# An FFT-style convolution on one core: 32-pixel x chunks, a first weight group from one weight copy, earlier plane bursts, and one queue for the last scratch reads

## The chip, the cores and the metric

The kernel runs on one core of a Trainium2 chip. The metric is the device time of one execution in microseconds (us). A program on one core has no second die to compare with, so a run counts as slow when it is over 1.5% above the fastest run of the same kernel, and only the fast runs are compared. Each profile is one further execution with the hardware profiler on; its span is some 1 to 2 us shorter than the timed runs.

## The reference

The reference is a circular 7x7 convolution done with Fourier transforms.

```
x: [1, 224, 224, 96] bfloat16      w: [7, 7, 96, 96] bfloat16
wp = pad(w, to 224 x 224)
Xf = rfft2(x as float32, axes=(1, 2));  Wf = rfft2(wp as float32, axes=(0, 1))
Yf = einsum('bhwi,hwio->bhwo', Xf, Wf)
y  = irfft2(Yf, s=(224, 224), axes=(1, 2)) as bfloat16
```

## The kernel before

The kernel transforms along the rows only, in blocks of 28 rows with a real transform of 34 points (17 frequencies). Along the other axis it convolves directly. Its stages are these:

- **x banks.** Rows of x (tile `xn`) are multiplied by a transform matrix `Fm` on TensorE, and the result is copied to `xf` (96 channels on partitions). The width is cut into seven tiles of 32 pixels, t = 0 to 6.
- **Weight banks.** w (tile `wq`) is multiplied by `Em` and copied to `WF`. This is done in six groups of frequencies. `wq` holds two copies of w on 49 partitions each, shifted by half the output channels. One matmul on 98 partitions then makes two output channels. The third weight slot of each frequency is the difference of the other two, formed on VectorE (`w_sub`).
- **Planes.** VectorE forms sums and differences of `xf` (tile `J`) for three frequencies at a time. Such a burst is `jit(t, g)`. There are two plane buffers, and a third in the two-tile phase.
- **Rounds.** `b_round(t, s)` runs 33 convolution matmuls of 96 columns (22 for frequency 0), combines them on ACT, VectorE and POOL (`u`, `v`, `yf`) and writes to a scratch tensor in DRAM (`scr`).
- **Output products.** The scratch is read back (`tt`), multiplied by the inverse matrix `Gm`, copied to `yo` and written out.

Tiles 0 and 1 run interleaved, tile 1 four rounds behind (the two-tile phase). Tiles 2 to 6 follow one by one. Other stages' matmuls are slipped into the rounds as "jobs", each list with a window of slots, two slots to a round. The parts that the change touches, with cuts marked:

```python
NXN = 4                                   # x buffers, each PXC = 16 pixels (of each phase pair) wide
# ... start: what is loaded, in program order; DE is the SP queue
load_rows(xh_bufs[0], 0, W - PAD, PAD)
load_x(0)
load_rows(xh_bufs[1], 1, W - PAD, PAD)
load_x(1)
load_w(0, DE)                             # first copy of w
for c in range(2, NXN):
    load_x(c)
# ... 24 warm matmuls; later, after the sine tables have been started:
load_w(1, SE)                             # second copy of w, from the ACT queue
# ... a weight bank of any group, the first one (full) included
for k in range(hb):                       # hb = 4
    o = ob * hb + k
    TE.matmul(pv_[:, k], lhsT=wqx[0:PW2, o:o + 127 * C + 1:C], rhs=ev, start=True, stop=True)
# ... the order of work at the start
a0 = a_jobs(0)                            # 28 x banks
p0 = prep_jobs(0)                         # 12 weight banks
for _ in range(16):
    a0.pop(0)()
warm(2)
for _ in range(4):
    p0.pop(0)()
while p0 or a0:
    if p0:
        p0.pop(0)()
    for _ in range(2):
        if a0:
            a0.pop(0)()
for f in jit(0, 0):
    f()
# ... when weight differences and plane bursts are formed in the two-tile phase
for gi in range(1, len(PGRP)):
    b0 = PGRP[gi][0]
    add(max(0, 2 * b0 - 10), 2 * b0 - 4 if gi > 1 else 2, prep_jobs(gi))
    for h, (r, t) in enumerate(((b0 - 4, 1), (b0 - 2, 0)) if gi > 1 else ((0, 0), (1, 0))):
        wsubs.setdefault((r, t if r >= LAG else 0), []).append(w_sub(gi, h))
for g in range(len(JGB)):
    g0 = JGB[g][0]
    # ...
    r1 = LAG + g0 - 1
    bursts[(r1, 0 if r1 < NS else 1)] = (1, g)
bursts[(NS + LAG - 1, 1)] = (2, 0)        # first planes of tile 2, in the very last round
for r in range(NS + LAG):
    if r == NS:
        add(2 * r, 2 * (r + LAG) - 2, a_jobs(2))
    # ...
    now = jit(*now) if now else []
    if (r, t) in wsubs:
        now.extend(wsubs.pop((r, t)))     # planes first, then weight differences
# ... tiles 2 to 6: the older tile's output products start in slot 3
km = 3 + -(-(k1 - 3) * nold // (nold + nnew))
add(3, km, cj[:nold])
# ... after the last round
load_b(1, SE, 1)
load_b(2, DE, 1)
```

## Time and profile before

| | before |
|---|---|
| runs, us | 304.72, 305.99, 301.41 (median 304.72) |
| span of the profiled execution | 301.7 us |
| mean granted TensorE clock | 0.954 |
| TensorE busy | 271.0 us (90%) |

The lines that carry the reading stand in the prediction below. To read them, start from the busy row and the clock row of the slices. Where TensorE has a gap, look at the clock just behind it. Then ask the list of TensorE's waits who ended the gap. Nearly every instruction carries the line of one helper (L82), so the groups are told apart by tile names, not by lines. The moment at which the convolution could first start ends the expensive start of this kernel. It is seen in the instructions in order of time (start, duration, engine, line, operation, tiles and form, and in brackets the idle time before and who ended it):

```profile
19.40 1.85 PE L82 MATMUL pb<-wq 98*128 98x100 bf16 x20 [6.63 <-DMA wq<-in_w_dram]
...
27.69 0.50 PE L82 MATMUL pb<-WF,xf 96*128 96x96 bf16 x8 [0.76 <-DVE WF L82]
```

The first weight product waits 6.63 us for w, and round 0 of the convolution starts at 27.69 us.

### The profile page before, as it was taken

What the parts mean: (1) busy time and instruction counts of PE and PEld (TensorE: products, weight loads), DVE (VectorE), ACT (ScalarE), POOL (GpSimd) and SP (SyncE); (2) the same over time, 40 slices, a digit from 0 to 9 for tenths busy, and PEclk for the clock granted to TensorE, in tenths of its full rate; (3) what the DMA queues carried; (4) which work ended last, traced back from release to release, by engine and by line L of the source; (5) the groups of instructions that cost most, each with busy time, mean ns of one, the idle gap of its engine ahead of it and who ended that gap; (6) DMA issues with size and microseconds to landing.
All of it is one profiled execution on the core that took longest, in us unless ns stands there. A gap on an engine that the chain in (4) does not pass through costs nothing. (4 is left out here: it accounts for less than half of the span.)

```text
span 301.7 us, 11617 instructions
## 1 busy us (share of the span) xinstructions
PE 271.0 (90%) x4826; PEld 244.3 (81%) x4826; DVE 241.6 (80%) x517; ACT 188.6 (62%) x466; POOL 88.4 (29%) x124
## 2 busy tenths in 40 slices
PE   8548969999989689999999999999999999899863
PEld 3448969999979688998989897989888988688742
DVE  7828998999898858788988889788988799578713
ACT  2427957665612744777688857878688864666113
POOL 6811001322434311322422423422423416222100
PEclk9958979999979977999999999999999999799999
DMA  7983223111121549877757773887549543957825
GB/s 184 187 194 99 54 72 112 41 41 43 42 81 41 169 132 206 230 204 215 215 169 193 212 211 125 230 232 200 166 135 220 145 137 105 242 168 189 196 79 182
DMA packets 46084, 46.01 MB, mean 152 GB/s; under 512 B 33658, under 2 KB 35238, under 8 KB 45934
## 3 DMA queue, kind: packets, MB, share of 16 engines
q1 hardware_dynamic: 44462, 42.61, 51.9%
q10 hardware_dynamic: 1570, 2.67, 3.3%
q8 instruction: 38, 0.62, 0.9%
q14 instruction: 14, 0.11, 0.1%
HBM read 23.92 MB, written 21.33 MB: 150 GB/s over the span
## 5 line engine op out<-in xcount | busy, mean ns | idle before, releaser
L82 PE MATMUL pb<-WF,J 96*128 96x96 bf16 x2898 | 172.9, 209 | 6.1 <-DVE J L82 5.6
L82 PEld LDWEIGHTS <-J 96*128 96x128 bf16 (+1 forms) x2910 | 147.3, 99 | 22.2 <-issue 10.1
L82 POOL TENSOR_TENSOR yf<-v,u 128x384 bf16<-128x384 f32 x74 | 74.2, 1017 | 176.9 <-issue 103.9
L82 ACT CAST xf<-pb 96x408 bf16<-96x408 f32 (+1 forms) x138 | 61.2, 468 | 12.8 <-PE pb L82 9.8
L82 ACT CAST yo<-pb 84x384 bf16<-84x384 f32 (+1 forms) x139 | 59.5, 479 | 9.5 <-PE pb L82 8.6
L82 PE MATMUL pb<-WF,xf 96*128 96x96 bf16 x952 | 61.6, 209 | 4.1 <-DVE WF L82 3.5
L82 DVE TENSOR_TENSOR J<-xf 96x1824 bf16<-96x1824 bf16 (+1 forms) x84 | 57.1, 719 | 0.0
L82 PEld LDWEIGHTS <-xf 96*128 96x128 bf16 x952 | 48.5, 99 | 4.5 <-issue 3.6
L82 PE MATMUL pb<-Fm,xn 118*128 118x136 bf16 x448 | 49.7, 233 | 1.2 <-DVE u L82 0.8
L82 PE MATMUL pb<-tt,Gm 102*84 102x384 bf16 (+1 forms) x144 | 36.8, 334 | 2.1 <-DMA tt<-scr 1.5
L82 ACT CAST WF<-pb 96x480 bf16<-96x480 f32 (+1 forms) x57 | 28.6, 563 | 10.3 <-PE pb L82 10.2
L82 PEld LDWEIGHTS <-xn 118*128 118x128 bf16 x448 | 32.3, 103 | 2.3 <-issue 1.9
L82 PE MATMUL pb<-wq 98*128 98x120 bf16 (+1 forms) x288 | 24.6, 236 | 6.8 <-DMA wq<-in_w_dram 6.6
L82 PEld LDWEIGHTS <-wq 98*128 98x128 bf16 x288 | 21.6, 151 | 7.3 <-issue 7.3
L82 DVE TENSOR_TENSOR J<-J 96x912 bf16<-96x912 bf16 (+1 forms) x42 | 25.0, 596 | 0.0
L82 DVE TENSOR_TENSOR yf<-v,u 128x384 bf16<-128x384 f32 x37 | 21.2, 572 | 1.3
L82 DVE CAST xf<-pb 96x408 bf16<-96x408 f32 (+1 forms) x34 | 16.3, 508 | 1.2 <-PE pb L82 0.8
L82 PEld LDWEIGHTS <-Gm 102*84 102x84 bf16 (+1 forms) x144 | 11.5, 115 | 4.4 <-DMA tt<-scr 1.6
L82 DVE CAST WF<-pb 96x480 bf16<-96x480 f32 (+1 forms) x15 | 9.0, 615 | 7.4 <-PE pb L82 7.2
L82 PE MATMUL pb<-wu 128*128 128x512 bf16 (+1 forms) x52 | 12.0, 392 | 1.1 <-DVE ct L82 1.1
L82 PEld LDWEIGHTS <-wu 128*128 128x128 bf16 (+1 forms) x52 | 6.2, 122 | 6.9 <-issue 3.4
L82 DVE CAST tt<-pb 112x384 bf16<-112x384 f32 x8 | 4.2, 554 | 8.2 <-PE pb L82 7.9
(390 smaller groups left out, 216.0 us busy)
## 6 DMA issues: line engine op xcount, KB each, us to landing
xn<-in_x_dram SPq DMA_DIRECT2D x28, 336.0 KB
scr<-yf SPq DMA_DIRECT2D x30, 288.0 KB
tt<-scr SPq DMA_DIRECT2D x24, 288.0 KB
out_dram<-yo SPq DMA_DIRECT2D x24, 252.0 KB
tt<-scr SPq DMA_DIRECT2D x12, 192.0 KB
out_dram<-yo SPq DMA_DIRECT2D x12, 168.0 KB
scr<-yf SPq DMA_DIRECT2D x6, 192.0 KB
wq<-in_w_dram SPq DMA_DIRECT2D x1, 864.0 KB
```

The costliest lines, as they stand in the source:

```text
L82: r = fn(*a, **k)
```

## The change

Its intent is to shorten the start (half the weight bytes before the first weight product), to take waits on `WF` and `J` out of the two-tile phase, and to free the ACT queue of a scratch read at the end. The diff, cut to its core (VectorE's copy into `Fm` also moves ahead of the second sine, and the x banks are cut from the wider chunks):

```diff
-NXN = 4
+NXN = 2                                   # two buffers of 32 pixels
 ...
 load_rows(xh_bufs[0], 0, W - PAD, PAD)
 load_x(0)
+load_w(0, DE)
 load_rows(xh_bufs[1], 1, W - PAD, PAD)
-load_x(1)
-load_w(0, DE)
-for c in range(2, NXN):
-    load_x(c)
+load_x(1, 0, 1)
+load_x(1, 1, 1)
+load_w(1, DE)                             # second copy last, same queue
 ...
-    for _ in range(8):                    # 24 warm matmuls
+    for _ in range(4):                    # 12
 ...
-GE.memset(wqx[0:PW2, C * C + 2 * NSLOT * NTAP:], 0.0)
-load_w(1, SE)
+SE.copy(out=wpad, in_=wu[0:PW2, 0:1].to_broadcast(list(wpad.shape)))
 ...
+if full:                                  # first group: 49 partitions, 8 matmuls of 50 columns a bank
+    ev = Em[0:PW, 0, ...]
+    for k in range(NB):
+        TE.matmul(pv_[:, k], lhsT=wqx[0:PW, o:o + 127 * C + 1:C], rhs=ev, start=True, stop=True)
 ...
-for _ in range(16): a0.pop(0)()
-warm(2)
-for _ in range(4): p0.pop(0)()
-while p0 or a0: ...
-for f in jit(0, 0): f()
+for _ in range(14): a0.pop(0)()
+for _ in range(4):
+    p0.pop(0)()
+    warm(1)
+for k in range(14):
+    a0.pop(0)()
+    if k in (6, 9): p0.pop(0)()
+for f in jit(0, 0): f()
+while p0:
+    p0.pop(0)()
+    if len(p0) % 2: warm(1)
 ...
-for h, (r, t) in enumerate(((b0 - 4, 1), (b0 - 2, 0)) ...
+for h, (r, t) in enumerate(((max(b0 - 4, 2), 1), (b0 - 2, 0)) ...
 r1 = LAG + g0 - 1
+if g == len(JGB) - 1:
+    r1 = NS                               # tile 1's last burst: round 18 -> 17
-bursts[(NS + LAG - 1, 1)] = (2, 0)
+bursts[(NS + LAG - 2, 1)] = (2, 0)        # tile 2's first burst: round 20 -> 19
-add(2 * r, 2 * (r + LAG) - 2, a_jobs(2))
+add(2 * r, 2 * (r + LAG - 2) + 1, a_jobs(2))
-now.extend(wsubs.pop((r, t)))
+now = wsubs.pop((r, t)) + now if r < 2 else now + wsubs.pop((r, t))
 ...
-km = 3 + -(-(k1 - 3) * nold // (nold + nnew))
-add(3, km, cj[:nold])
+k0 = 12 if t == 2 else 3
+km = k0 + -(-(k1 - k0) * nold // (nold + nnew))
+add(k0, km, cj[:nold])
-load_b(1, SE, 1)
+load_b(1, DE, 1)
```

More of the change, by code (lines that the diff above doesn't have):

```diff
@@ L146 @@
     assert sum(KB) == 128
-    xn_bufs = [cpool.tile([R, PXC * C + 32], BF16, name=f"xn{i}") for i in range(NXN)]
+    xn_bufs = [cpool.tile([R, 2 * PXC * C + 32], BF16, name=f"xn{i}") for i in range(NXN)]
     wtmp_cm = tc.tile_pool(name="wtmp", bufs=1, side="right")
@@ L159, with load_rows @@
     for xb in xn_bufs:
-        GE.memset(xb[:, PXC * C:], 0.0)
+        GE.memset(xb[:, 2 * PXC * C:], 0.0)
     for xb in xh_bufs:
         GE.memset(xb[:, PAD * C:], 0.0)
-    def load_rows(xb, jg, w0, npx):
+    def load_rows(xb, jg, w0, npx, b0=0):
         h0 = jg * HB - PAD
@@ L168, in ld, with load_x @@
         def ld(p0, p1, hh):
-            dma(xb[p0:p1, 0:n], x[0, hh:hh + (p1 - p0), w0:w0 + npx, :].rearrange("h w c -> h (w c)"))
+            dma(xb[p0:p1, b0 * C:b0 * C + n], x[0, hh:hh + (p1 - p0), w0:w0 + npx, :].rearrange("h w c -> h (w c)"))
         ld(PAD, R, h0 + PAD)
         ld(0, PAD, h0 % H)
-    def load_x(c):
-        t, k = divmod(c, 4)
-        h, jg = divmod(k, 2)
-        load_rows(xn_bufs[c % NXN], jg, t * 2 * TW + h * PXC, PXC)
+    def load_x(c, h0=0, nh=2):
+        t, jg = divmod(c, 2)
+        load_rows(xn_bufs[c % NXN], jg, t * 2 * TW + h0 * PXC, nh * PXC, h0 * PXC)
     wsrc = w.rearrange("kh kw i o -> (kh kw) (i o)")
-    NCH = 4 * NT
-    load_rows(xh_bufs[0], 0, W - PAD, PAD)
-    load_x(0)
-    load_rows(xh_bufs[1], 1, W - PAD, PAD)
-    load_x(1)
+    NCH = 2 * NT
     def load_w(h, eng):
@@ L186, in load_w @@
             eng.dma_start(out=wq[h * PW + p0:h * PW + p1, 0:C * C - h * C2], in_=wsrc[p0:p1, h * C2:])
+    load_rows(xh_bufs[0], 0, W - PAD, PAD)
+    load_x(0)
     load_w(0, DE)
-    for c in range(2, NXN):
-        load_x(c)
+    load_rows(xh_bufs[1], 1, W - PAD, PAD)
+    load_x(1, 0, 1)
+    load_x(1, 1, 1)
+    load_w(1, DE)
     wu = cpool.tile([128, 128], BF16, name="wu")
@@ L243 @@
     sin_q(qf[:])
-    load_w(1, SE)
+    wpad = wqx[0:PW2, C * C + 2 * NSLOT * NTAP:]
+    SE.copy(out=wpad, in_=wu[0:PW2, 0:1].to_broadcast(list(wpad.shape)))
     GE.affine_select(out=qf[:], in_=qf[:], pattern=[[-B, JG], [0, NS * 2]], compare_op=ALU.is_ge, fill=0.0, base=0, channel_multiplier=1)
@@ L255 @@
     VE.scalar_tensor_tensor(out=qe[:], in0=a3[:], scalar=thp[:, 0:1], in1=ph3[:], op0=ALU.mult, op1=ALU.add)
+    VE.tensor_copy(out=Fm.rearrange("p r s j -> p j s r"), in_=qf[:])
     sin_q(qe[:])
@@ L260 @@
     VE.tensor_tensor(out=mk2[:, 0], in0=mk[:], in1=mk2[:, 1], op=ALU.subtract)
-    VE.tensor_copy(out=Fm.rearrange("p r s j -> p j s r"), in_=qf[:])
     pe3 = ftile([PW2, NSLOT])
@@ L324, in f @@
                 pw = bank()
+                if full:
+                    pv_ = pw[:, 0:NB * ncol].rearrange("p (k q) -> p k q", k=NB)
+                    ev = Em[0:PW, 0, slot(s0, 0):slot(s0, 0) + ncol // NTAP, :].rearrange("p a t -> p (a t)")
+                    for k in range(NB):
+                        o = ob * NB + k
+                        TE.matmul(pv_[:, k], lhsT=wqx[0:PW, o:o + 127 * C + 1:C], rhs=ev, start=True, stop=True)
+                    wv = WF[0:C, slot(s0, 0):slot(s0, 0) + ncol // NTAP].rearrange("i a t o -> i (a t) o")
+                    apart(("W", gi), ob, evac(wv[..., ob * NB:(ob + 1) * NB], pv_[0:C].rearrange("i k q -> i q k"), NB * ncol))
+                    return
                 pv_ = pw[:, 0:NB * ncol].rearrange("p (k h q) -> p k h q", h=2, q=ncol)
-                if full:
-                    ev = Em[:, :, slot(s0, 0):slot(s0, 0) + ncol // NTAP, :].rearrange("p h a t -> p h (a t)")
-                else:
+                if True:
                     ev = Em[:, :, slot(s0, 0):slot(s1 - 1, 2) + 1, :].rearrange("p h (s r) t -> p h s (r t)", r=3)[:, :, :, 0:2 * NTAP]
@@ L334, in f @@
                 o0, o1 = ob * hb, (ob + 1) * hb
-                if full:
-                    wv = WF[0:C, slot(s0, 0):slot(s0, 0) + ncol // NTAP].rearrange("i a t (h o) -> i (a t) h o", h=2)
-                    apart(("W", gi), ob, evac(wv[..., o0:o1], pv_.rearrange("i k h q -> i q h k"), NB * ncol))
-                    return
                 wv = WF[0:C, slot(s0, 0):slot(s1 - 1, 2) + 1].rearrange("i (s r) t (h o) -> i s (r t) h o", r=3, h=2)
@@ L411, in a_jobs @@
         jobs = []
-        if t == 0:
-            for jg in range(2):
+        for jg in range(2):
+            if t == 0:
                 jobs.extend(a_bank(t, xf, xh_bufs[jg], 0, 3, jg, 0))
-        for k in range(4):
-            h, jg = divmod(k, 2)
-            c = 4 * t + k
-            for (q, n) in ((0, 3), (3, 3), (6, 2)):
-                jobs.extend(a_bank(t, xf, xn_bufs[c % NXN], 2 * q, n, jg, HALO + h * 8 + q))
+            c = 2 * t + jg
+            for h in range(2):
+                for (q, n) in ((0, 3), (3, 3), (6, 2)):
+                    jobs.extend(a_bank(t, xf, xn_bufs[c % NXN], h * PXC + 2 * q, n, jg, HALO + h * 8 + q))
             last = jobs.pop()
@@ L646 @@
     p0 = prep_jobs(0)
-    for _ in range(16):
+    for _ in range(14):
         a0.pop(0)()
-    warm(2)
     for _ in range(4):
         p0.pop(0)()
-    while p0 or a0:
-        if p0:
+        warm(1)
+    for k in range(14):
+        a0.pop(0)()
+        if k in (6, 9):
             p0.pop(0)()
-        for _ in range(2):
-            if a0:
-                a0.pop(0)()
     for f in jit(0, 0):
         f()
+    while p0:
+        p0.pop(0)()
+        if len(p0) % 2:
+            warm(1)
     g_fin()
@@ L689 @@
         add(max(0, 2 * b0 - 10), 2 * b0 - 4 if gi > 1 else 2, prep_jobs(gi))
-        for h, (r, t) in enumerate(((b0 - 4, 1), (b0 - 2, 0)) if gi > 1 else ((0, 0), (1, 0))):
+        for h, (r, t) in enumerate(((max(b0 - 4, 2), 1), (b0 - 2, 0)) if gi > 1 else ((0, 0), (1, 0))):
             wsubs.setdefault((r, t if r >= LAG else 0), []).append(w_sub(gi, h))
```

## The prediction

> **What bounds the kernel now.** I read the page's busy shares first, then the slices, then the busy times by stretch, then the waits of TensorE, and last the instructions in order of time around each wait.
>
> ```profile
> PE 271.0 (90%) x4826; PEld 244.3 (81%) x4826; DVE 241.6 (80%) x517; ACT 188.6 (62%) x466; POOL 88.4 (29%) x124
> ...
> PE   8548969999989689999999999999999999899863
> ...
> PEclk9958979999979977999999999999999999799999
> ```
>
> TensorE is busy 271.0 of 301.7 us, so only 30.7 us are idle. But the clock row has dips behind the dips of the PE row. The mean granted clock was 0.954, so about 0.046 x 301.7 = 13.9 us of full-speed work was lost to half clock as well. So what can be had is idle time plus the half clock behind it. The busy times by stretch (start:end, then PE, weight load, DVE, ACT, POOL, then clock, DMA share and GB/s) show where:
>
> ```profile
> 12.20:19.37 7.17, 0.58 (x4) 0.08 (x2) 1.66 (x5) 0.21 (x1) 3.65 (x11) 0.68 0.95 215
> 19.37:27.69 8.32, 7.38 (x80) 7.11 (x81) 6.00 (x12) 6.15 (x14) 0.15 (x1) 0.66 0.50 129
> 27.69:38.75 11.06, 10.84 (x187) 10.49 (x188) 10.80 (x22) 10.13 (x24) 1.10 (x1) 1.00 0.28 85
> 38.75:46.00 7.25, 4.51 (x58) 4.50 (x57) 6.32 (x12) 3.16 (x8) 0.10 (x1) 0.76 0.22 62
> 46.00:83.74 37.74, 37.63 (x800) 37.13 (x797) 34.82 (x69) 24.59 (x58) 11.77 (x12) 1.00 0.16 57
> 99.84:113.76 13.92, 9.35 (x156) 8.98 (x155) 9.81 (x22) 7.59 (x20) 2.61 (x5) 0.88 0.50 144
> 118.00:250.00 132.00, 130.69 (x2528) 117.97 (x2527) 111.96 (x235) 102.78 (x262) 42.02 (x43) 1.00 0.69 191
> ```
>
> From 46 to 84 and from 118 to 250 us TensorE is 99% busy at full clock; nothing is to be had there. It is lost at 12 to 28, at 39 to 46, at 84 to 90, at 100 to 118 and at both ends. TensorE's own waits name the releasers:
>
> ```profile
> PE pb L82 <- DMA wq<-in_w_dram: 6.6, 1, 6.6
> PE pb L82 <- DVE J L82: 5.6, 4, 1.9
> PE pb L82 <- DVE WF L82: 3.5, 2, 2.7
> PE pb L82 <- DMA xf<-scrb: 3.0, 1, 3.0
> ```
>
> The 6.6 us is the first weight product waiting for w. It reads 98 partitions, so it needs both copies of w. The second copy comes on the ACT queue and shares the 16 DMA engines with x chunks: the DMA share is 0.95 over 12.2 to 19.4 us. The instructions in order of time show what a wait leaves behind:
>
> ```profile
> 40.01 0.62 DVE L82 TENSOR_TENSOR J<-J 96x912 bf16<-96x912 bf16 x1
> 40.55 1.72 DVE L82 TENSOR_TENSOR WF<-WF 96x1440 bf16<-96x1440 bf16 x2
> 41.50 0.33 PE L82 MATMUL pb<-WF,xf 96*128 96x96 bf16 x4 [2.74 <-DVE WF L82]
> ...
> 105.57 0.34 PE L82 MATMUL pb<-WF,J 96*128 96x96 bf16 x4 [1.92 <-DVE J L82]
> ...
> 113.76 1.30 PE L82 MATMUL pb<-WF,J 96*128 96x96 bf16 x14 [1.90 <-DVE J L82]
> ```
>
> At 41.5 TensorE wants the weights' difference (WF), but VectorE did 2.0 us of planes (J) first. At 105.6 and 113.8 it wants planes formed only one round earlier. In the per-microsecond clock, 0.50 follows at 42.5 to 45.5, 107 to 110.5 and 114 to 117.
>
> **What the Trainium skill says.** "TensorE: Matmul & The Clock Gate", section "What's actually happening", gives two states, 4/8 and 8/8, set by a free-running window of 3413 ns. The trace agrees with the states (0.50 and 1.00) and the length: each half-clock spell here is about 3.4 us. It differs in the trigger. The page asks for an idle window, while here a window with 1.9 us idle was enough (103.65 to 105.57), and the one at 83.74 to 85.21 (1.47 us) too. A gap of 0.75 us at 100.6 left the clock at 1.00. So I charge a gap of 1.5 us or more with another 3.41 x 0.5 = 1.7 us.
> "DMA: Bandwidth & Descriptors", section "Issuing engines are not separate DMA queues", says that transfers issued from different engines interleave on the same 16 engines. The trace agrees: with both queues in flight at 12.2 to 19.4 us the core moved 215 GB/s at a DMA share of 0.95, so the second queue adds no bandwidth there. The order of bytes is what counts.
>
> **The change, part by part.**
>
> *Start.* Bytes before round 0 may begin: two x edges of 133 KB, tile 0's x (1,416 KB) and w. Before, both copies of w (1,760 KB) were needed; after, one (882 KB), loaded ahead of the second half of x. The rates of 174 and 215 GB/s average near 190. The first copy then lands after (133+708+882)/190 = 9.1 us, plus 2.3 us for the start of the first transfer and about 1 us for landing: 12.4 us instead of 19.4. The last of tile 0's x lands after 2.56 MB, 13.5 us, so at about 16.8 us. The second copy is last, 3.44 MB, about 21.5 us.
> TensorE pays for it. The first group goes from 48 matmuls to 96 of half the width. From the row of 32 wq matmuls in 2.18 us, one costs 68 ns, and with the wq load before each I don't expect 50 columns to be cheaper: 96 x 0.068 = 6.5 us instead of 3.3. In order: first 14 x banks until about 12.4 (28 banks, ACT and DVE empty one in about 0.25 us each between them), 4 weight banks with their warm matmuls 3.0 us, then 14 x banks and 2 weight banks, the last 6 x banks not before 16.8 us: about 20.2. Then 6 weight banks of 0.54 us and 3 warm ones of 0.21, 3.9 us, beside which VectorE forms the planes (1.58 + 0.62 us), and one copy of 0.5 us: round 0 at 24.2 to 24.6 instead of 27.69. **Gain 3.5 us.** Dropping 12 warm matmuls frees nothing; they ran while x was in flight. The 1.82 us memset that moves from POOL to ACT lies beside the x load.
>
> *Tile 1's x.* 32-wide chunks in two buffers hold as many bytes as four of 16. The second pair follows the second w copy: about 25.5 and 29 us. Its consumers come at about 26.5 and 32 (before, less 3.5). Just hidden.
>
> *Weight differences ahead of planes in rounds 0 and 1.* At 41.5 TensorE then waits for one WF subtraction (0.9 us) instead of 1.40 + 0.62 + 0.9. The gap falls from 2.74 to about 0.8 and should not cost the clock: 1.9 + 1.7 = 3.6. VectorE is busy 6.32 of 7.25 us there, so I take **3.0**.
>
> *Plane bursts a round earlier.* The two gaps of 1.92 and 1.90 us and their half clocks, 3.8 + 3.4 = 7.2. The last tile-1 burst has a whole round more and vanishes. The first burst of tile 2 takes 2.0 us after the last x bank is emptied, against one round of 43 matmuls (1.75 us) and a short lead-in; I leave 0.7 us of wait. Denser x banks, 5 per slot instead of 4, cost about 1.0. **Gain 5.5.**
>
> *Output products of tile 0 from slot 12 instead of 3.* The scratch reads can't start before TensorE has left the third plane buffer, and early rounds would now run at full clock into them. It moves work later; rounds 0 to 5 get thin and VectorE-bound: **minus 0.5.**
>
> *Last scratch read on SP.* It only changes which transfer goes first near 285 us; the last write (4.81 us from 285.03 in the chain) is what ends. **0.**
>
> Sum: 3.5 + 3.0 + 5.5 - 0.5 = 11.5 us. Base 304.0, between the profiled run's 303.45 and the median 304.72: **292.5 us.**
>
> **The rivals.** (1) *VectorE keeps the time.* Between 46 and 83.74 it is 34.82 of 37.74 us busy. If the delayed work meets it again, only idle at the gaps moves and the waits on J return elsewhere, say at 84 us. Then 3 to 5 us are given back: 296 to 298. For it: the four waits on J. Against it: TensorE was 99% busy there. (2) *DMA stays the bound of the start.* If the second w copy and tile 1's x land late, round 0 stops at its first wide weight banks, with a half clock after it: the start gains nothing, 296. For it: DMA share 0.95. Against: it needs them some 3 us after they are due. (3) *The clock decides more.* The startup gap of 7 us vanishes, and the clock at 19 to 25 us was 0.50; if every gap left is under 1.5 us, also at 84 us, gains reach 15 us: 289. (4) *Fewer warm matmuls bring half clock early*: from about 4.6 to 7.3 us TensorE would be idle. That slows x banks that wait for w anyhow.
>
> **Range and chances.** The base itself ran from 301.4 to 306.0. Rivals 1 and 2 give 296 to 298 each, 3 gives 289. Range 288 to 298. A gain over 2% needs less than 298.6: 0.90; within 2%: 0.09; slower: 0.01.
>
> **What would show it.** First WF matmul near 12.5 us; round 0 near 24; no wait on DMA wq over 1.5 us; the gap at round 2 under 1.2 us and clock 1.00 after it; no waits on J over 1 us in the last four rounds before tile 2; the gaps at 84 and 258 us still there; the end from the last convolution on (282.5 to 301.7) still about 19 us. I am wrong if TensorE's busy time rises by more than the 3 us of extra weight matmuls, or if new gaps of over 1.5 us stand between 46 and 118 us.

## The result and the profile after

The changed kernel took 294.44 us (median of 4 runs, 293.81 to 295.94). The kernel before, in the same rounds, took 304.48. A ratio here is the mean time of one kernel's fast runs over the mean of the other's fast runs of the same rounds, so it isn't quite the ratio of the medians. It is 0.971, with a 95% interval of 0.9626 to 0.9795. That is faster by 2.9%, inside the predicted range and 1.9 us above the predicted time. The page of the changed kernel (busy times, then the rows of 40 slices):

```profile
PE 269.9 (92%) x4867; PEld 242.5 (83%) x4867; DVE 240.8 (82%) x516; ACT 190.5 (65%) x469; POOL 84.6 (29%) x120
...
PE   6399999999979889999999999999999999899873
...
PEclk9958699999989999999999999999999999999998
```

The mean clock rose from 0.954 to 0.967. Up to the last convolution matmul, half-clock spells are now 14.1 to 20.9, 27.7 to 34.5 and 85.7 to 89.1 us. Before there were six: 14.8 to 25.0, 42.1 to 45.5, 86.4 to 89.9, 106.9 to 110.3, 113.8 to 117.2 and 260.5 to 263.9. TensorE's waits in the trace of the changed kernel (total, times, longest, in us):

```profile
PE pb L82 <- DVE J L82: 4.4, 6, 1.5
PE pb L82 <- DMA wq<-in_w_dram: 4.0, 1, 4.0
...
PE pb L82 <- DVE WF L82: 1.0, 2, 0.6
```

The waits on `WF` shrank from 3.5 to 1.0 us and those on w from 6.6 to 4.0. But the idle time that left isn't the gain. To see where time went I used the records of the 3,850 matmuls that read `WF`. Their order is the same in every version, so the start of the n-th one is a mark that can be set against the same mark elsewhere. Three marks lie inside their rounds: "middle of round 5" and "round 17" stand 11 matmuls into these rounds, "round 8 of tile 2" 22. Stretches between marks, in us:

| from the start of | to | before | after | difference |
|---|---|---|---|---|
| the span | round 0 | 27.69 | 28.39 | +0.70 |
| round 0 | round 1 | 6.81 | 8.78 | +1.97 |
| round 1 | round 3 | 11.73 | 8.27 | -3.46 |
| round 3 | middle of round 5 | 6.34 | 7.41 | +1.07 |
| middle of round 5 | round 17 | 45.04 | 45.13 | +0.09 |
| round 17 | round 8 of tile 2 | 34.29 | 27.29 | -7.00 |
| round 8 of tile 2 | round 2 of tile 6 | 119.66 | 120.54 | +0.88 |
| round 2 of tile 6 | round 8 of tile 6 | 15.94 | 14.02 | -1.92 |
| round 8 of tile 6 | last convolution matmul | 14.99 | 15.12 | +0.13 |
| last convolution matmul | end | 19.24 | 17.89 | -1.35 |

The differences sum to -8.9 us, which is the difference of the spans (301.75 and 292.84 before rounding). They compare one trace with one trace, half-clock spells included. **The start lost 2.7 us** where 3.5 us were predicted as gain. The stretch with the bursts gained 7.0. The instructions in order of time in the changed kernel:

```profile
14.14 0.65 PE L82 MATMUL pb<-wq 49*128 49x50 bf16 x8 [4.00 <-DMA wq<-in_w_dram]
...
28.39 0.80 PE L82 MATMUL pb<-WF,xf 96*128 96x96 bf16 x8 [0.57 <-ACT WF L82]
...
41.91 0.33 PE L82 MATMUL pb<-WF,xf 96*128 96x96 bf16 x4 [0.47 <-DVE WF L82]
...
85.58 0.39 PE L82 MATMUL pb<-WF,J 96*128 96x96 bf16 x4 [1.49 <-DVE J L82]
...
109.26 0.77 PE L82 MATMUL pb<-WF,J 96*128 96x96 bf16 x14 [0.73 <-DVE J L82]
...
253.23 0.49 PE L82 MATMUL pb<-tt,Gm 102*84 102x384 bf16 x2 [1.19 <-DVE J L82]
```

The first weight product starts 5.3 us sooner (14.14 against 19.40), and yet round 0 starts 0.7 us later. The waits at rounds 2 (41.91) and before tile 2 (109.26) are down to 0.47 and 0.73 us as predicted. The one at 85.58 stayed.

The stretches of the start in busy times (start:end, length, then PE, weight load, VectorE, ACT and POOL busy with counts, then granted clock, DMA share, GB/s) show what became of the 5.3 us:

```profile
10.13:14.14 4.01, 0.01 (x2) 0.04 (x1) 1.86 (x5) 0.64 (x3) 3.35 (x11) 0.99 0.88 170
14.14:28.39 14.25, 13.68 (x141) 10.61 (x142) 7.95 (x15) 7.32 (x17) 0.78 (x2) 0.74 0.73 181
...
24.30:27.71 3.41, 3.41 (x43) 2.85 (x42) 2.57 (x5) 1.77 (x4) 0.00 (x0) 1.00 0.77 215
27.71:31.12 3.41, 2.83 (x32) 2.83 (x32) 1.32 (x4) 2.08 (x5) 0.36 (x1) 0.50 0.02 5
31.12:34.54 3.42, 3.42 (x38) 3.42 (x37) 2.83 (x5) 2.10 (x4) 0.00 (x0) 0.50 0.00 0
```

From 14.14 to 28.39 us TensorE is busy for 13.68 of 14.25 us, so the start is no longer a wait, it is work. And there is a puzzle: the window 24.30 to 27.71 is busy all the time, and the clock halves right behind it for two windows.

### The profile page after: what moved, and what is told of

It is laid out like the page before. It is cut to its first block, busy times and chain, and to the rows that moved or that the text cites. A ratio compares the mean times of both kernels' runs of the same rounds, so it can differ in the third digit from the quotient of the medians.

```text
span 292.8 us, 11651 instructions
## 1 busy us (share of the span) xinstructions
PE 269.9 (92%) x4867; PEld 242.5 (83%) x4867; DVE 240.8 (82%) x516; ACT 190.5 (65%) x469; POOL 84.6 (29%) x120
## 3 DMA queue, kind: packets, MB, share of 16 engines
q10 hardware_dynamic: 720, 1.47, 1.4%
## 4 chain that ended last, share of the span: by engine, by line
PE 53%; DVE 30%; DMA 7%; issue 4%; ACT 2%; POOL 2%; SPq 1%; ACTq 0%; DVEq 0%; POOLq 0%
PE pb L82 53%; DVE J L82 10%; DVE v L82 6%; DVE xf L82 4%; DVE yf L82 4%; DMA wq<-in_w_dram 4%; DVE u L82 3%; DVE WF L82 2%; POOL yf L82 2%; ACT WF L82 1%; DMA scrb<-yf 1%; DMA scr<-yf 1%; DMA xf<-scrb 1%; SPq L82 1%; ACT tt L82 0%
## 5 line engine op out<-in xcount | busy, mean ns | idle before, releaser
L82 PE MATMUL pb<-WF,J 96*128 96x96 bf16 x2898 | 169.8, 207 | 3.6 <-DVE J L82 3.2
L82 PEld LDWEIGHTS <-J 96*128 96x128 bf16 (+1 forms) x2910 | 144.7, 98 | 20.5 <-issue 10.3
L82 ACT CAST xf<-pb 96x408 bf16<-96x408 f32 (+1 forms) x141 | 62.2, 469 | 9.0 <-PE pb L82 6.0
L82 PE MATMUL pb<-Fm,xn 118*128 118x136 bf16 x448 | 46.9, 228 | 2.2 <-DMA xn<-in_x_dram 1.5
L82 PEld LDWEIGHTS <-xn 118*128 118x128 bf16 x448 | 30.8, 101 | 2.9 <-DMA xn<-in_x_dram 1.6
L82 PE MATMUL pb<-wq 98*128 98x120 bf16 (+1 forms) x336 | 27.9, 233 | 4.0 <-DMA wq<-in_w_dram 4.0
L82 PEld LDWEIGHTS <-wq 98*128 98x128 bf16 (+1 forms) x336 | 24.5, 153 | 6.6 <-issue 6.3
L82 DVE CAST xf<-pb 96x408 bf16<-96x408 f32 (+1 forms) x31 | 14.8, 512 | 2.5 <-PE pb L82 2.3
L82 PEld LDWEIGHTS <-Gm 102*84 102x84 bf16 (+1 forms) x144 | 11.4, 114 | 4.3 <-DMA tt<-scr 1.3
L82 PE MATMUL pb<-wu 128*112 128x384 bf16 (+1 forms) x45 | 12.1, 405 | 1.1 <-DVE ct L82 1.1
L82 PEld LDWEIGHTS <-wu 128*112 128x112 bf16 (+1 forms) x45 | 5.5, 124 | 5.6 <-issue 3.0
```

What stands on the lines that cost most here:

```text
L82: r = fn(*a, **k)
```

## The experiments

All kernels here gave a correct result. They ran in three calls of four; the kernels of one call share a chip and the runs of the kernel before. All variants are changed kernels with one thing undone, or the kernel before with some parts done. I put forward these theories:

1. The start is worth nothing or less, and the gain comes from the later parts. Rival: the start pays, and the profile caught a bad execution.
2. The half clock after a busy window comes from few columns and partitions being streamed. Rival: TensorE was idle in ways that the page hides.
3. The late output products (slot 12) cost a little, as I had predicted. Rival: the bursts can't work without them.

### Parts alone

**The start alone**: the changed kernel with bursts, windows, output products, order of differences and the last read put back.

```diff
-r1 = NS  (for the last g)      +(removed)
-bursts[(NS + LAG - 2, 1)]      +bursts[(NS + LAG - 1, 1)]
-add(2 * r, 2 * (r + LAG - 2) + 1, a_jobs(2))   +add(2 * r, 2 * (r + LAG) - 2, a_jobs(2))
-k0 = 12 if t == 2 else 3       +k0 = 3
-load_b(1, DE, 1)               +load_b(1, SE, 1)
-wsubs.pop((r, t)) + now        +now + wsubs.pop((r, t)), and max(b0 - 4, 2) -> b0 - 4
```

> The kernel before with only the start changed (32-wide chunks, one weight copy for the first group, its loads and warm matmuls). Theory, from the trace after: the start gains nothing; round 0 begins near 28.4 us instead of 27.7 and round 1 about 2.7 us late because the clock is at half from 28 to 35 us; some of it is taken back at round 2, where VectorE is late anyway. Time: 0 to +2.5 us against before. Rival (my prediction): the start gains 3.5 us, so -3.5. The weight product should start near 14 us in either case.

Measured: 301.54 us, ratio 0.9954 (0.9905 to 1.0003), against 302.92 for the kernel before. The start alone is worth about half a per cent, and the interval reaches no gain at all. In its trace round 1 starts at 37.62 us, against 34.50 before, and yet its span is 2.1 us shorter. Its later stretches show where that comes from. From round 17 to round 8 of tile 2, where its code is that of the kernel before but for the wider x chunks, it takes 32.26 us instead of 34.29: the two waits on `J` are there again (1.92 and 1.90 us), but no half clock follows them. And from round 2 of tile 6 to the end it takes 47.35 us instead of 50.18. The two waits in order of time, then the busy times around them (full clock throughout):

```profile
108.34 0.34 PE L82 MATMUL pb<-WF,J 96*128 96x96 bf16 x4 [1.92 <-DVE J L82]
114.93 0.77 PE L82 MATMUL pb<-WF,J 96*128 96x96 bf16 x14 [1.90 <-DVE J L82]
```

```profile
102.00:119.00 17.00, 11.44 (x226) 10.70 (x224) 14.32 (x31) 9.98 (x27) 3.17 (x5) 1.00 0.67 180
```

**The bursts alone**: the kernel before with the two bursts a round earlier, their x window and slot 12.

```diff
+if g == len(JGB) - 1: r1 = NS
-bursts[(NS + LAG - 1, 1)]      +bursts[(NS + LAG - 2, 1)]
-add(2 * r, 2 * (r + LAG) - 2, a_jobs(2))   +add(2 * r, 2 * (r + LAG - 2) + 1, a_jobs(2))
+k0 = 12 if t == 2 else 3
```

> The kernel before with only the last plane bursts a round earlier, the x banks of tile 2 in five slots less one, and the output products of tile 0 from slot 12. Theory: nearly the whole gain sits here: the gap between the convolution matmuls number 979 and 1177 shrinks by 6 to 7 us, time -6 to -7.5 us (a further -2 if the half clock at 258 us is gone as well). Rival (my prediction's share): -5.0 us.

Measured: 298.04 us, ratio 0.9834 (0.9784 to 0.9883). From round 17 to round 8 of tile 2 its trace takes 27.29 us, exactly as the changed kernel's. So the gain in that stretch belongs to this part. How much of the 7.0 us is the waits themselves: against the start alone, which has the same waits without half clock, it is 5.0 us. The other 2.0 are half clock that the trace of the kernel before happened to have, and not every execution has it.

**Everything but the start**: the kernel before with bursts, slot 12, differences first and the last read on SP.

```diff
 (the edits of the bursts alone, and)
-now.extend(wsubs.pop((r, t)))
+now = wsubs.pop((r, t)) + now if r < 2 else now + wsubs.pop((r, t))
-((b0 - 4, 1), ...   +((max(b0 - 4, 2), 1), ...
-load_b(1, SE, 1)    +load_b(1, DE, 1)
```

> Everything of the change but the start: weight differences first, bursts, slot 12, last scratch on one queue. Theory: as the start of the changed kernel loses 2.7 us by round 1, this one is at round 3 some 3.5 us ahead of before and not worse than the changed kernel at the end: 0 to -3 us against the changed kernel (291.5 to 294.5). If VectorE holds rounds 3 to 13, as rival 1 said, most of these 3.5 us are given back by 98 us and the two are equal within 1 us.

Measured: 294.13 us, ratio 0.9701 (0.9654 to 0.9747). The whole change gave 0.971. So no gain of the new start is seen in a mean of several runs either; the intervals, about half a per cent to each side here and nearly one there, leave room for a small one. In six traces with the new start round 1 begins at 37.2 to 39.2 us (changed kernel twice, the start alone, and the variants with the last read on ACT, with slot 3 and with planes first; mean 38.0). In four with the old start it begins at 34.5 to 36.0 (mean 35.3). By traces the new start costs 2.7 us up to there. The same traces give it back at the other end: from round 2 of tile 6 to the end the ten traces with the new start take 45.8 to 47.7 us (mean 46.7), the four with the old one 48.3 to 50.2 (mean 49.4). So the two cancel. The wide x chunks, which this part brings for all tiles, are one candidate, half clock by chance another (leaving out the spell that ends every trace, it is in that stretch in three of the four old ones and one of the ten new ones); no run tells them apart.

**The last read on ACT**: the changed kernel with that one line put back.

```diff
-load_b(1, DE, 1)
+load_b(1, SE, 1)
```

> The changed kernel with the read of the second-last scratch back on the ACT queue. Theory: with the read on the same queue behind the last write, the write's packets go first, which is where 1.4 us of the tail came from (4.81 us down to 3.21 us for the last write). Back on ACT: +1.0 to +1.5 us. Rival (my prediction): 0.

Measured: 295.33 us, ratio 0.9737 (0.9683 to 0.9791), beside 0.971 and 0.9722 for the change: no difference that the intervals allow to be seen. From the last convolution matmul to the end four traces with the ACT queue take 18.09 to 19.24 us, and ten with SP take 16.86 to 20.04. This part isn't resolved; its value is less than the scatter. The old or new start parts these traces better than the queue does: 18.60 to 20.04 us with the old one, 16.86 to 18.43 with the new one.

### Slot 12

The changed kernel with tile 0's output products back in slot 3.

```diff
-k0 = 12 if t == 2 else 3
+k0 = 3
```

> The changed kernel with the output products of tile 0 from slot 3 of tile 2 again. Theory (of the prediction's step): the scratch reads can only be issued once TensorE has left the third plane buffer, so the first product now waits for them 1 to 3 us at full clock, with a half clock behind it: +2 to +4 us against the changed kernel. Rival: the wait is hidden by the other work of the slot, and moving the products later is what cost 0.5 us: -0.5 to 0.

Measured: 301.57 us, ratio 0.9974 (0.9892 to 1.0055). Nearly the whole gain of the change is gone. I had expected a loss of 2 to 4 us, and it is 7 to 8. The instructions in order of time of this variant (the second line is a wait of TensorE, the first the scratch reads on the SP queue), and its busy times between:

```profile
114.73 5.81 SPq L82 DMA_DIRECT2D tt<-scr  x10
...
118.83 0.84 PE L82 MATMUL pb<-tt,Gm 102*84 102x384 bf16 x2 [4.53 <-DMA tt<-scr]
```

```profile
114.48:117.90 3.42, 0.00 (x0) 0.00 (x0) 3.42 (x7) 0.36 (x1) 0.13 (x1) 1.00 0.73 186
```

With the bursts a round earlier, TensorE comes to tile 2 before the scratch of tile 0 has been read. The first product in slot 3 stands in TensorE's order ahead of the convolution, so TensorE does nothing for 4.53 us. Two windows at half clock follow (117.9 to 124.7). The stretch from round 17 to round 8 of tile 2 takes 35.30 us, longer than the 34.29 of the kernel before. So slot 12 is no cost beside the gain; without it the earlier bursts gain nothing in that stretch. Slot 12 without the earlier bursts wasn't run.

### The clock at the start

These variants add TensorE work around the last weight banks, to see what the clock needs. The first adds matmuls of 512 columns on 128 partitions, the second matmuls of 50 columns.

```diff
 p0.pop(0)()
-if len(p0) % 2:
-    warm(1)
+warm(3)
```

> The changed kernel with 18 warm matmuls of 512 columns instead of 3 among the last six narrow weight banks. Theory: the half clock from 28 to 35 us follows a window in which TensorE is 100% busy by the profile but streams columns for only some 45% of it, as a 50-column matmul takes 72 ns; with the warm ones it streams over 60%, and the clock stays 1.00 until round 1. The added 3.2 us and the saved 3 us about cancel: round 0 at 31 to 32 us, round 1 within 1.5 us of the changed kernel. Rival: the 0.57 us of idle ahead of round 0 or the phase sets it, and the half clock stays: round 1 some 3 us later than in the changed kernel.

Measured: 298.59 us over four runs, of which two are slow (301.65 and 305.84); the fast ones are 294.53 and 295.54, ratio 0.9747 (0.9641 to 0.9852).

```diff
 p0.pop(0)()
 if len(p0) % 2:
     warm(1)
+narrow(8)      # 8 matmuls, lhsT=wu[:, 0:128], rhs=wu[:, 0:50]
```

> The changed kernel with 48 further matmuls of 50 columns, reading a constant, among the same six weight banks: about as much added TensorE time as the 15 added warm ones, but few columns. If the columns streamed set the clock, it goes to half in this stretch, from 24 to 28 us on, and round 1 is 4 to 6 us later than in the changed kernel. If busy time sets it, the clock stays 1.00 as with the warm matmuls.

Measured: 297.26 us, ratio 0.9821 (0.9734 to 0.9908). The busy times of the two windows in question, first the variant with wide warm matmuls:

```profile
25.97:29.39 3.42, 3.42 (x29) 1.88 (x27) 0.89 (x3) 1.43 (x3) 0.00 (x0) 1.00 0.55 178
29.39:32.80 3.41, 3.41 (x37) 2.26 (x36) 1.13 (x3) 0.88 (x4) 0.36 (x1) 1.00 0.00 0
```

Then the variant with narrow ones:

```profile
25.67:29.09 3.42, 3.42 (x60) 2.92 (x59) 1.37 (x4) 1.46 (x3) 0.00 (x0) 1.00 0.55 190
29.09:32.50 3.41, 3.28 (x47) 3.07 (x43) 1.49 (x4) 1.47 (x4) 0.36 (x1) 0.50 0.00 0
```

Both first windows are busy throughout, 3.42 of 3.42 us. Behind the wide matmuls the clock stays at 1.00, behind twice as many matmuls, most of them narrow, it falls to 0.50. So busy time doesn't decide it. From the records of the matmuls I counted columns x partitions read in each window, as a share of what 128 partitions at 2.4 columns per ns would take (matmuls of 512 columns follow each other every 0.215 us at full clock, which is this rate). A matmul that crosses the edge of a window counts in each by its time there, as the profile models it. The share is 0.234 in the changed kernel's window at 24.30 us, 0.353 in the window with narrow matmuls and 0.553 with wide ones.

Over 14 traces a line at 0.374 parts the windows: under it half clock follows, above it full clock, for all but 2 of 1,171 windows, both within 0.005 of the line. The best line by busy time alone misses 48, by columns alone 18. Fitted without the two traces above, the line lies at the same place, between 0.374 and 0.379, and puts both their windows on the right side. I take the share as a description that fits, not as a proven mechanism: no run varied the partitions by themselves.

The wide warm matmuls cost what they save. Round 0 starts at 32.16 us and round 1 at 38.56, 1.4 us after the changed kernel's 37.17, as expected. The narrow ones put round 1 at 38.95; I had expected 4 to 6 us more than the changed kernel, and it was 1.8.

The third variant fills the wait for w instead:

```diff
 for _ in range(14):
     a0.pop(0)()
+warm(14)
 for _ in range(4):
     p0.pop(0)()
```

> The changed kernel with 14 warm matmuls in the wait for the first weight copy (10.1 to 14.1 us). Theory: the clock is 1.00 instead of 0.50 from 14 to 21 us, the first four weight banks take 3.0 instead of 4.4 us and the x banks behind them less, round 0 comes 1.5 to 2.5 us sooner (26 to 27 us); the half clock after 28 us stays. Rival: TensorE is not what this stretch waits for, the last x chunk is: round 0 within 0.5 us.

Measured: 293.08 us, ratio 0.9701 (0.9611 to 0.9791), no different from the change. Round 0 starts at 28.88 us where I had expected 26 to 27: a miss, and the outcome of the rival (within 0.5 us of the changed kernel's 28.39). The half-clock spells only moved, to 8.4 to 11.9, 18.7 to 22.1 and 25.5 to 32.3 us. The window of narrow weight matmuls ahead of the second spell (15.27 to 18.68 us) is fully busy at a share of 0.365, under the line: filling the gap doesn't make the work behind it less thin. That the last x chunk sets this stretch, as the rival said, isn't excluded.

### Differences first, and two attempts at a better kernel

The changed kernel was run again for comparison.

```diff
 (no edit: the changed kernel)
```

> The changed kernel once more, on the same chip as the three others of this set: 294 us, within 1 us of its first result.

Measured: 296.22 us, ratio 0.9722 (0.9681 to 0.9763). Its trace has half clock from 12.8 to 36.7 us, and round 0 starts at 30.30 us against 28.39 in the first one. The start of the same kernel thus varies by 1.9 us from one execution to the next.

**Planes first again**: the changed kernel with the old order of planes and weight differences.

```diff
-((max(b0 - 4, 2), 1), ...
+((b0 - 4, 1), ...
-now = wsubs.pop((r, t)) + now if r < 2 else now + wsubs.pop((r, t))
+now = now + wsubs.pop((r, t))
```

> The changed kernel with the planes ahead of the weight differences in round 1 again, and the second group's first difference back in round 1. Theory: the gap of 2.7 us at round 2 comes back with its half clock, round 3 is 3 to 3.5 us later than in the changed kernel; 1.1 us of that is given back by the wait near 51 us, so +2 to +2.5 us at the end.

Measured: 297.12 us, ratio 0.9757 (0.9704 to 0.9809). That is 0.4% (some 1.1 us) over the changed kernel beside it, with intervals that overlap. The trace is clearer: the wait at round 2 is back.

```profile
44.88 0.33 PE L82 MATMUL pb<-WF,xf 96*128 96x96 bf16 x4 [2.33 <-DVE WF L82]
```

From round 1 to round 3 it takes 11.37 us against 8.26, and from there to the middle of round 5 6.34 against 7.40. So 3.1 us are gained and 1.1 given back: about 2.0 remain.

**The old start with the gap at 84 us covered**: everything but the start, and five warm matmuls before the round that waits on `J` there.

```diff
 both = LAG <= r < NS
+if (r, t) == (13, 1):
+    warm(5)
 b_round(...)
```

> The kernel with the old start and the rest of the change, with 5 warm matmuls ahead of the convolution that waits for planes at 84 us. Theory: the columns times partitions streamed in that window stay over the share at which the clock was halved in the ten traces so far (0.37 to 0.38 of what 128 partitions could do at full clock), so the half clock from 86 to 89 us is gone for good: 1.0 to 1.7 us less by the convolution matmul number 979 than in the same kernel without them, unless VectorE is what holds this stretch, when it is 0. Time 292.5 to 294.

Measured: 295.46 us, ratio 0.9692 (0.9639 to 0.9746). No half clock at 84 us is left. That the warm matmuls did it isn't shown, as three kernels without them had none there either. But the stretch didn't become shorter. The busy times from the middle of round 5 to round 17, first of the kernel before:

```profile
52.58:97.62 45.04, 43.19 (x908) 42.60 (x907) 42.15 (x87) 22.12 (x52) 15.40 (x16) 0.96 0.13 49
```

Then of this variant:

```profile
50.81:95.95 45.14, 42.90 (x912) 41.40 (x911) 42.21 (x87) 22.13 (x52) 15.41 (x16) 1.00 0.13 49
```

The clock is 0.96 in one and 1.00 in the other, and both take 45.1 us. VectorE is busy for 42.2 of them in both. In 13 of the 14 traces this stretch takes 45.04 to 45.15 us, eight of them with one window at half clock and five with none; the fourteenth (slot 3) had two in a row and took 46.44. So one such window costs nothing here. That VectorE sets the length is what its busy time speaks for; no run made VectorE's work shorter.

**Weights ahead of x**: the changed kernel with the first w copy loaded ahead of the first x chunk, weight banks ahead of x banks, 12 warm matmuls before them, and the five at round 13.

```diff
+load_w(0, DE)
 load_x(0)
-load_w(0, DE)
 ...
-for _ in range(14): a0.pop(0)()
-for _ in range(4): p0.pop(0)(); warm(1)
+for _ in range(2): a0.pop(0)()
+warm(12)
+for _ in range(4): p0.pop(0)(); warm(1)
+for _ in range(6): p0.pop(0)(); warm(1); a0.pop(0)(); a0.pop(0)()
 for k in range(14):
     a0.pop(0)()
-    if k in (6, 9): p0.pop(0)()
+    if k in (4, 9): p0.pop(0)()
```

> The changed kernel with the first weight copy loaded ahead of tile 0's pixels, 12 warm matmuls in the wait for it, ten weight banks ahead of or between the first x banks with a warm matmul each, and the 5 warm ones at 84 us. Theory: the narrow weight banks then fill the time in which TensorE waited for the x loads, and none stand between the last x bank and round 0: round 0 at 25 to 26.5 us instead of 28.4, clock 1.00 through round 1, and at round 3 some 2 to 4 us ahead of the changed kernel; of that VectorE's stretch up to 98 us may keep half. Time 290 to 292.5. Rival: the last x chunk and the copies out of PSUM set round 0, and it stays at 28.

Measured: 294.94 us, ratio 0.9678 (0.9632 to 0.9724). Round 0 starts at 31.94 us where I had expected 25 to 26.5, with half clock from 12.9 to 30.0 us: a miss. Both attempts lie 0.3 to 0.45% under the changed kernel of the same call, with overlapping intervals. No version is shown to beat the changed kernel.

## Why the prediction was right or wrong

Right: 294.44 us against 292.5, in the range of 288 to 298, and faster by over 2%. But the sum was right by luck, because errors cancelled. By its own steps, with the differences of the two traces:

| step | predicted | measured |
|---|---|---|
| start, to round 1 | -3.5 | +2.7 |
| differences first | -3.0 | -3.5, then 1.1 given back: -2.4 |
| bursts and slot 12 together | -5.5 + 0.5 = -5.0 | -7.0, then 0.9 given back: -6.1 |
| gap at 258 us | stays, 0 | -1.9 (rounds 2 to 8 of tile 6) |
| the end | 0 | -1.35 |
| the rest | 0 | +0.2 |
| sum | -11.5 | -8.9 |

- **Start: the step failed.** The prediction put round 0 at 24.2 to 24.6 us; it came at 28.39. "The first copy then lands after (133+708+882)/190 = 9.1 us" and so at 12.4: the first product ran at 14.14, 1.7 us late. The rate was not far off: by 11.4 us, where the sum ends these transfers, 1.71 MB had been moved, and 1.76 MB were needed (the sum takes KB of 1,024 bytes as 1,000, which is 0.2 us). But some of it was the next x load, and the load of w goes out as 48 rows and a 49th by itself. The 48 had landed by 13.1 us; the single packet of the 49th (18 KB) started only at 11.7 and ended at 13.0, and its semaphore came at 14.0. "4 weight banks with their warm matmuls 3.0 us" took 4.4, at half clock from 14.1 to 20.9. The x banks with two weight banks took 5.5, not 4.8. The last six banks and the copy took 4.4, as predicted (3.9 and 0.5; the sum 20.2 + 3.9 + 0.5 is 24.6, so by its own terms the gain was 3.1 rather than 3.5). After that I had counted nothing: half clock from 27.7 to 34.5 added 2.0 us between rounds 0 and 1. I had taken the size of a narrow matmul right (68 ns; it took 68 to 72), but not what such matmuls do to the clock.
- **Rival 2** ("the start gains nothing") had the outcome. Its cause was right in part only: w did land late, but no wide weight bank waited for the second copy. The larger share is thin TensorE work at half clock. That the start's loss hardly appears in the times of whole runs (0.971 with it, 0.9701 without) fits the 2.7 us that the same traces give back from round 2 of tile 6 on. Why they do stays open, and the start varies by 1.9 us between two executions of one kernel.
- **Rivals 3 and 4.** The clock didn't bring the 15 us of rival 3: the mean rose from 0.954 to 0.967 only. Rival 4 (half clock early with fewer warm matmuls) came in four of the ten traces with the new start, from 7.8 to 8.9 us on, in none of the four with the old one, and not in the changed kernel's own.
- **Differences first: right in mechanism and nearly in size.** The gap fell from 2.74 to 0.47 us and the clock stayed up, as predicted. What I missed is the 1.1 us that returned two rounds later, as the planes now come later.
- **Bursts: right in mechanism.** Both waits went (0.73 us left of 1.92 and 1.90, where I had put 0.7), with their half clocks. That the -7.0 is larger than predicted isn't shown: against the start alone, whose waits cost no half clock, the stretch is 5.0 us shorter. "Minus 0.5" for slot 12 was the wrong reading: the gain depends on it. Without it the stretch takes 35.30 us instead of 27.3.
- **The charge of 1.7 us for a half clock** behind each gap of 1.5 us holds only where a half clock follows and TensorE sets the time. In the start alone gaps of 1.92 and 1.90 us left the clock at 1.00. ("Each half-clock spell here is about 3.4 us" was misread too: the one at the start, 14.8 to 25.0, is three windows long.) At 84 us a half clock was there or not, and the stretch took 45.1 us. Rival 1 ("VectorE keeps the time") is true of that stretch, though not where I had placed its cost.
- **The gap at 258 us** was said to stay. In the changed kernel the product there waits 1.19 us and the clock stays at 1.00. Before, it waited 1.47 and lost a window. Runs with the old x chunks took 14.2 to 16.1 us for this stretch, those with the wide ones 13.8 to 14.2. The longest two (15.9 and 16.1) held a half clock, the rest none. Whether the chunks or the phase of the clock window decide that wasn't tested.
- **The end** was shorter by 1.35 us in this pair of traces. The variants don't confirm that the queue did it.
- **What was to show it.** First weight product near 12.5 us and round 0 near 24: wrong, 14.14 and 28.39. No new gap over 1.5 us from 46 to 118: right, the longest is 1.49. The wait on w of at most 1.5 us: wrong, 4.0. The gap at round 2 under 1.2 us with full clock after it: right. No wait on `J` over 1 us in the last four rounds: right. The gap at 84 us still there: right. TensorE's busy time not up by over 3 us: right, it fell by 1.1.

## What to carry to other kernels

Halving the bytes that a first product waits for moves its start, but not the stage behind it, if the work becomes thinner on the way; in these traces columns x partitions streamed, and not busy time, told when half clock followed. Try each part of a bundled change alone and in pairs: here one part showed no gain, and another gained only together with a delay that looked like a cost. Before a gap's half clock is counted as lost time, look whether another engine sets the length of that stretch.

## What the Trainium skill lacked or had wrong

- "TensorE: Matmul & The Clock Gate", section "What's actually happening", names an idle window of about 3.4 us as what brings the half clock. Here it also came behind windows in which TensorE was busy 3.41 of 3.41 us, with 43 matmuls (24.30 to 27.71 us). A share of columns x partitions under about 0.374 of the full rate describes it, with 2 exceptions in 1,171 windows. That section doesn't mention partitions.
- The same section has one busy window bring the full clock back. In the second run of the changed kernel three windows in a row (16.2 to 26.4 us) were fully busy, at shares of 0.27 to 0.35, and the clock stayed at half; one at 0.41 (33.2 us) brought it back. A window full of convolution matmuls on 96 partitions at half clock has a share of 0.376 to 0.383, just above the line: at 84 to 91 us the clock came back behind nine of ten such windows and stayed at half behind one (slot 3, 87.18 us, 0.377). The section's remark that the ramp varies from run to run agrees with this.
- The same page, section "Back-to-back issue gap", gives about 60 cycles for matmuls of 1 to 64 columns, as an isolated gap, and says that with a weight load before each the spacing is set by both; it has no number for so few columns with weight loads. Eight matmuls of 50 columns with weights read at a stride (every 96th element, 49 partitions) took 0.58 us, 73 ns each. Eight of 50 columns on 128 partitions with weights in a row took 0.30 us, 38 ns each, in the same window of the variant with narrow matmuls (start of one group to start of the next):

```profile
25.18 0.64 PE L82 MATMUL pb<-wq 49*128 49x50 bf16 x8
25.76 0.37 PE L82 MATMUL pb<-wu 128*128 128x50 bf16 x8
26.06 0.67 PE L82 MATMUL pb<-wq 49*128 49x50 bf16 x8
```

  That the stride makes the difference wasn't tested by itself; the partitions differ as well. The weight loads take 156 ns each in the one and 96 in the other.
- "Perfetto Trace Analysis", section "Identifying the Most-Contended Engine", says that matmul busy time is a bad measure of how near TensorE is to its roofline. The runs agree (100% busy at a share of 0.23). No page that I read says the converse for the clock: a stretch in which VectorE was 94% busy took 45.04 and 45.14 us at mean clocks of 0.96 and 1.00.
